# A two-layer spectral and dense block on one core: input rows spread over three DMA queues, the last slot of the spectral stage in halves of columns, and group 6's inverse steps moved ahead of the last group's third step

## The chip, the core and the metric

The kernel runs on one core of a Trainium2 chip. The metric is device time in microseconds (us) for one execution, taken as the median of several runs. Engines are named as in the profile: PE is TensorE, PEld its weight load, DVE VectorE, ACT ScalarE, POOL GpSimd, SP SyncE. SPq and ACTq are the DMA issues of SP and ACT.

## The reference

The input x has 2048 tokens of 1024 values. Two layers follow each other, each made of a spectral part A and a dense part B, with a layer norm ahead of each part and a residual after it:

```python
def _A_ref(x, w_r, w_i):
    B, S, D = x.shape
    X = rfft2(x.astype(float32))
    W = w_r + 1j * w_i
    return irfft2(X * W, s=(S, D)).astype(bfloat16)

def _B_ref(x, w1, b1, w2):
    h = einsum("bsd,df->bsf", x, w1) + b1
    sp = log1p(exp(-abs(h))) + where(h > 0, h, 0)
    return einsum("bsf,fd->bsd", h * tanh(sp), w2)

x = x + _A_ref(_layernorm(x), w_r, w_i)
x = x + _B_ref(_layernorm(x), w1, b1, w2)
x = x + _A_ref(_layernorm(x), w_r, w_i)
x = x + _B_ref(_layernorm(x), w1, b1, w2)
```

Here w_r and w_i are 2048 x 513, w1 is 1024 x 3584 and w2 is 3584 x 1024.

## The kernel before, in words

Every instruction is recorded by a small scheduler in Python: an engine has a list in the order in which the instructions are written, and waits are worked out from who wrote and read which buffer. So the order on an engine is the order of the source, and a wait holds everything behind it on that engine. DMAs (helper line L251) are issued by SP, ACT or POOL; the waits of a DMA hold the issuing engine.

**Prologue and s1.** SP issues the token tiles of x (XS, 13 transfers, one of them on ACT) and then x a second time in another layout, XR. XR has its rows in four quarters q of 32 column blocks; each quarter is eight transfers (h = 0 to 7) of 16 partitions x 32 runs of 256 bytes, 128 KB each. Even h is issued by SP, odd h by POOL after the last but two of the token tiles has landed. Meanwhile DVE and ACT compute the statistics of the layer norm (L471, L474, L452); a square root on ACT (`root`, L443) and a small transpose on PE (L595) turn them into scale factors. The matrix of the first transform step is then multiplied by these factors in 16 parts j, on ACT for j = 1 (L610), on POOL for j = 2, 4, 9, 10, 11, 13 and on DVE for the others (L616). Step s1 follows (L635): part j is eight matmuls into a pair of PSUM banks, which ACT (L641) or DVE (L643) copies out. Part j needs quarter j // 4 of XR. Three pairs of banks rotate. In the second layer, s1 takes another way to its rows and the prologue's transfers don't occur.

**The spectral steps.** The work is cut into eight groups g with two slots each. The steps of a group are 2 (`s2`, L742), 3 (`s3`, L787 to L790: four matmuls, a scaled copy on ACT at L794, and four DVE operations at L798, L800, L803, L805 that multiply by the filter), 4 (`i1`, L816: eight matmuls, copy out at L827) and 5 (`i2`, L841 and L873: copy out by ACT at L885 or DVE at L883). `order_A` writes the order of all steps by hand as three-digit words: step, group, slot or half. "371" is step 3 of group 7, slot 1. Each step takes the next of four pairs of PSUM banks in turn.

**The bounce through DRAM.** After both halves of step 5, `u_turn` writes the group's result to a scratch tensor (SP, 512 KB) and a later call reads it back with rows and columns exchanged (`u_back`, 16 partitions x 128 runs of 256 bytes, issued by SP). For group 7, each half is written by ACT as soon as it is there; `u_last` reads it back in six transfers: two of 8 partitions for the first half (SP), and four of 8 partitions, one for each quarter q, for the second half (q = 0, 2 on ACT; q = 1, 3 on SP).

**After the last step.** PE runs four `spin` matmuls (L652), eight matmuls of the residual (L1033) and a number of `hold` matmuls on a zero operand (L657; 16 in the first layer, 11 in the second), and then the last inverse step `i4` (L1044) quarter by quarter, each with a wait on that quarter's rows. Layer norm and the dense part (L1154, L1193, L1233, L1332) come after it.

Of the kernel before, what the change touches and what calls it, by code (L numbers as in the profile page):

```python
# [5 lines left out]
ACT = mybir.ActivationFunctionType  # L6
ALU = mybir.AluOpType
P = 128
# [172 lines left out]
class KB:  # L181
# [200 lines left out]
    def prologue(self):  # L382
        sp = self.sp
        self.op(self.pool, lambda e: e.memset(self.EPS[:], 1e-5), writes=[self.r_eps, self.r_warm])
        xt = self.x[0].rearrange("(t p) d -> p t d", p=P)

        for a, b in ((10, 11), (0, 1), (1, 2), (11, 12), (2, 3), (3, 4), (12, 13), (4, 6), (13, 14), (6, 8), (14, 15), (8, 10), (15, 16)):
            self.dma(self.act if a == 10 else sp, self.XS[:, a:b, :], xt[:, a:b, :], f"x{a}", writes=self.r_xs[a:b])
        self.warm(ACT.Sqrt)
        small = {}  # L390
        def load_small(name, n, d):
            b = self.alloc(name, self.o[name], [n], d)
            self.dma(sp, b.ap, self.con[name], name.lower(), writes=[b.res])
            small[name] = b
        load_small("M0", P, BF)
        load_small("IDF", P, F32)
        self.M0, self.IDF = small["M0"], small["IDF"]

        self.XR = self.alloc("XR", self.o["XR"], [P, P])
        self.r_xr = []  # L400
        xv = self.x[0].rearrange("(n2 n1) (h l) -> h n2 n1 l", n2=16, l=P)
        for q in range(4):
            r = Res(f"xr{q}")
            for h in range(8):
                prog = self.pool if h % 2 else sp
                self.dma(prog, self.XR.ap[h:P:8, 32 * q:32 * q + 32, :], xv[h][:, 32 * q:32 * q + 32, :], f"xr{q}{prog.name}",
                         parts=[r], reads=[self.r_xs[13]] if prog is self.pool else [])
            self.r_xr.append(r)
        self.dma(sp, self.FD[:], self.con["FD"], "fd", writes=[self.r_fd])
        load_small("JT", 4 * P, BF)  # L410
        self.JT, self.r_jt = small["JT"].ap, small["JT"].res
        self.w1_next = 0
# [168 lines left out]
    def first_scales(self):  # L581


        dve, act = self.dve, self.act
        for j in range(10):
            self.stats_dve(j)
        for j in range(10, 16):
            self.stats_act(j)
        self.sums_to_mv(10, 6)
        self.root(0, 16)  # L590
        rt = self.alloc("RT", self.o["RT"], [16, 8], F32)
        self.op(dve, lambda e: e.tensor_copy(rt.ap, self.RS[:, 2, :].unsqueeze(2).to_broadcast([P, 16, 8])),
                reads=self.r_rs, writes=[rt.res])
        bank = self.r_bank[7]
        self.group([lambda e: e.transpose(self.PS[:, 7, 0:P], rt.ap.rearrange("p a b -> p (a b)"), self.IDF.ap)],  # L595
                   reads=[rt.res, self.IDF.res], writes=[bank])
        self.op(dve, lambda e: e.tensor_copy(rt.ap.rearrange("p a b -> p (a b)"), self.PS[:, 7, 0:P]), reads=[bank], writes=[rt.res])
# [63 lines left out]
    def ring(self, name, n, size, shape):  # L661
        return [self.alloc(f"{name}{i}", self.o[name] + size * i, shape) for i in range(n)]
# [49 lines left out]
    def layer_A(self, li):  # L712
# [18 lines left out]
        def zslot(g, i):  # L731
            return Z[(2 * g + i) % 6]
# [48 lines left out]
        def s3(g, i):  # L781

            ps, banks, _ = self.pair()
            z, ft = zslot(g, i), FT[g % 3]
            t = ft.ap[:, i, :]
            fns = [
                lambda e: e.matmul(ps[:, 0:512], t[:, 0:128], z.ap[:, 0, :], start=True, stop=False),  # L787
                lambda e: e.matmul(ps[:, 512:1024], t[:, 0:128], z.ap[:, 1, :], start=True, stop=False),
                lambda e: e.matmul(ps[:, 512:1024], t[:, 128:256], z.ap[:, 0, :], start=False, stop=True),
                lambda e: e.matmul(ps[:, 0:512], t[:, 256:384], z.ap[:, 1, :], start=False, stop=True),  # L790
            ]
            self.group(fns, reads=[z.res, ft.res], writes=banks)
            x = X[(2 * g + i) % 4]
            self.op(act, lambda e: e.activation(x.ap.rearrange("p a b -> p (a b)"), ps, ACT.Copy, scale=SIG),  # L794
                    reads=banks, writes=[x.res])
            wt, yk = WT[(2 * g + i) % 8], YK[(2 * g + i) % 6]
            ta, tb = T[2 * i], T[2 * i + 1]
            self.op(dve, lambda e: e.tensor_tensor(ta.ap, x.ap, wt.ap[:, 0:1, :].to_broadcast([P, 2, 512]), ALU.mult),  # L798
                    reads=[x.res, wt.res], writes=[ta.res])
# [5 lines left out]
            self.op(dve, lambda e: e.tensor_tensor(yk.ap[:, 1, :], tb.ap[:, 0, :], ta.ap[:, 1, :], ALU.add),  # L805
                    reads=[ta.res, tb.res], parts=[yk.res])

        def i1(g, i):

            ps, banks, _ = self.pair()  # L810
            yk, bt, v = YK[(2 * g + i) % 6], BT[g % 3], V[g % 2]
            t = bt.ap[:, i, :]
            fns = []
            for c in range(4):
                for part in range(2):
                    fns.append(lambda e, c=c, part=part: e.matmul(  # L816
                        ps[:, c * 256:(c + 1) * 256], yk.ap[:, part, c * P:(c + 1) * P], t[:, (128, 0)[part]:(384, 256)[part]],
                        start=(part == 0), stop=(part == 1)))
            self.group(fns, reads=[yk.res, bt.res], writes=banks)
# [96 lines left out]

        def u_last():

            def back(prog, half, q, n):
                l = slice(32 * q, 32 * q + 32 * n)  # L920
                self.dma(prog, self.UT.ap[7 + 64 * half:P if half else 64:8, l, :], self.u_d[7][l, 8 * half:8 * half + 8, :].rearrange("l r n -> r l n"),
                         f"ul{half}{q}", reads=[self.r_ud7[half]], parts=self.r_ut[q:q + n])
            back(sp, 0, 0, 2)
            back(sp, 0, 2, 2)
            for q in range(4):
                back((act, sp)[q % 2], 1, q, 1)

        self.s1(li)
        if li:
# [5 lines left out]
        T = ring("T", 4, 2 * K, [2, 512])  # L935
        YK = ring("YK", 6, 2 * K, [2, 512])
# [41 lines left out]
    @staticmethod  # L978
    def order_A():


        order = ("200 201 210 211 300 301 220 310 400 221 311 401 230 320 410 500 231 321 411 501 330 331 420 510 240 511 421 241 "
                 "250 251 340 341 520 350 430 260 521 431 440 261 351 441 530 531 360 361 270 450 451 271 540 541 550 551 460 370 "
                 "461 371 560 561 470 471 570 571")
        return [tuple(map(int, w)) for w in order.split()]

    def load_wr(self, wr, g):
# [798 lines left out]
```

## Time and profile before

| | us |
|---|---|
| median of 3 runs (lowest, highest) | 928.16 (926.5, 930.47) |
| profiled span | 924.9 |
| PE busy | 878.7 (95%) |
| DVE busy | 622.9 (67%) |
| ACT busy | 434.8 (47%) |
| POOL busy | 157.5 (17%) |
| granted TensorE clock, mean | 0.998 |

Busy shares are averages over stages with different limits. Three stretches are touched by the change: the first 37 us, and the end of the spectral stage in each layer (about 85 to 112 us and 536 to 562 us from the span's start). In a timeline, each row gives the start, the busy time, the engine, the line, the operation, the number of instructions merged in the row, and in brackets how long the engine had been idle before it and what released it. In the chain of waits, each row gives the start, the length and the engine or transfer that set the pace. In the list of one line's instructions, the three numbers are shortest, median and longest duration in ns.

### The profile page before, as it was taken

What the parts mean: (1) busy time and instruction counts of PE and PEld (TensorE: products, weight loads), DVE (VectorE), ACT (ScalarE), POOL (GpSimd) and SP (SyncE); (2) the same over time, 40 slices, a digit from 0 to 9 for tenths busy, and PEclk for the clock granted to TensorE, in tenths of its full rate; (3) what the DMA queues carried; (4) which work ended last, traced back from release to release, by engine and by line L of the source; (5) the groups of instructions that cost most, each with busy time, mean ns of one, the idle gap of its engine ahead of it and who ended that gap; (6) DMA issues with size and microseconds to landing.
All of it is one profiled execution on the core that took longest, in us unless ns stands there. A gap on an engine that the chain in (4) does not pass through costs nothing.

```text
span 924.9 us, 13613 instructions
## 1 busy us (share of the span) xinstructions
PE 878.7 (95%) x5503; PEld 470.5 (51%) x5503; DVE 622.9 (67%) x987; ACT 434.8 (47%) x643; POOL 157.5 (17%) x186
## 2 busy tenths in 40 slices
PE   0899899999999999999998998999999999999998
PEld 0677576444444444444456766754444444444443
DVE  7898468686789667568867765666747655554463
ACT  7998475456103485520018966757550025552000
POOL 5831003960004651010121200000000000000000
PEclk9999999999999999999999999999999999999999
DMA  9979862674786388363723786345165635732432
GB/s 298 294 236 288 208 175 66 212 276 121 279 271 240 134 318 300 121 230 141 285 92 109 225 220 158 137 166 182 32 198 187 206 136 187 273 120 84 175 124 107
DMA packets 145919, 175.99 MB, mean 190 GB/s; under 512 B 66904, under 2 KB 124472, under 8 KB 145736
## 3 DMA queue, kind: packets, MB, share of 16 engines
q1 hardware_dynamic: 132960, 128.49, 44.6%
q0 software_dynamic: 10800, 45.00, 13.5%
q10 hardware_dynamic: 2096, 1.64, 0.6%
q8 instruction: 43, 0.70, 0.3%
q14 instruction: 20, 0.16, 0.1%
HBM read 130.78 MB, written 40.89 MB: 186 GB/s over the span
## 4 chain that ended last, share of the span: by engine, by line
PE 86%; DVE 6%; ACT 5%; DMA 2%; issue 1%; SPq 0%; ACTq 0%; DVEq 0%
PE PS L1332 37%; PE PS L1233 30%; PE PS L1193 6%; PE PS L742 3%; PE PS L816 2%; ACT ARENA L452 2%; PE PS L841 2%; PE PS L1044 2%; DMA ARENA<-u_scratch 1%; ACT ARENA L641 1%; PE PS L1154 1%; PE PS L652 1%; DMA u_scratch<-ARENA 1%; DVE ARENA L798 1%; DVE ARENA L800 1%; PE PS L873 1%
## 5 line engine op out<-in xcount | busy, mean ns | idle before, releaser
L1332 PE MATMUL PS<-ARENA 128*128 128x512 bf16 x1568 | 340.1, 379 | 0.0
L1233 PE MATMUL PS<-ARENA 128*128 128x512 bf16 (+1 forms) x1288 | 280.3, 379 | 0.8 <-DVE ARENA L1238 0.8
L1332 PEld LDWEIGHTS PS<-ARENA 128*128 128x128 bf16 x1568 | 153.2, 98 | 184.7 <-DMA ARENA<-in_B_w_dram 0.4
L1238 DVE TENSOR_TENSOR ARENA<-PS,ARENA 128x512 f32<-128x512 f32 x230 | 157.1, 691 | 100.4 <-PE PS L1233 92.6
L1233 PEld LDWEIGHTS PS<-ARENA 128*128 128x128 bf16 x1288 | 125.5, 98 | 153.1 <-DVE ARENA L1238 3.5
L1243 ACT ACTIVATE ARENA<-ARENA,B 128x512 bf16<-128x512 f32 x138 | 98.8, 721 | 69.1 <-DVE ARENA L1238 63.8
L574 ACT ACTIVATE ARENA<-PS 128x512 f32<-128x512 f32 (+3 forms) x86 | 61.6, 726 | 110.7 <-PE PS L1233 92.4
L1126 POOL TENSOR_TENSOR ARENA<-ARENA 128x512 bf16<-128x512 bf16 x56 | 71.3, 1272 | 77.1 <-DVE ARENA L523 63.6
L452 ACT ACTIVATE ARENA<-XS 128x1024 bf16<-128x1024 bf16 x60 | 63.2, 1053 | 36.3 <-DVE XS L1383 33.0
L1193 PE MATMUL PS<-ARENA 128*128 128x256 bf16 (+1 forms) x528 | 75.0, 300 | 3.4 <-DVE ARENA L1159 1.9
L1357 DVE TENSOR_TENSOR ARENA<-ARENA 128x3584 bf16<-128x3584 bf16 x32 | 63.9, 2017 | 0.0
L1193 PEld LDWEIGHTS PS<-ARENA 128*128 128x128 bf16 x528 | 51.0, 99 | 23.0 <-DVE ARENA L1159 3.3
L1383 DVE TENSOR_TENSOR XS<-PS,ARENA 128x512 bf16<-128x512 f32 x52 | 35.7, 690 | 38.7 <-PE PS L1332 38.4
L1375 DVE TENSOR_TENSOR ARENA<-PS,ARENA 128x512 f32<-128x512 f32 x48 | 32.9, 688 | 27.4 <-PE PS L1332 27.0
L1197 ACT ACTIVATE ARENA<-PS,B 128x256 bf16<-128x256 f32 (+1 forms) x66 | 33.2, 515 | 30.3 <-PE PS L1193 30.2
L1243 ACT ACTIVATE ARENA<-PS,B 128x512 bf16<-128x512 f32 x46 | 31.5, 685 | 18.4 <-PE PS L1233 18.4
L1371 DVE TENSOR_TENSOR ARENA<-ARENA,XS 128x512 f32<-128x512 f32 x52 | 36.8, 732 | 0.5
L443 ACT ACTIVATE RS<-MV,EPS 128x1 f32<-128x1 f32 (+2 forms) x11 | 3.3, 296 | 71.5 <-DVE MV L565 70.1
L794 ACT ACTIVATE ARENA<-PS 128x1024 bf16<-128x1024 f32 x32 | 32.5, 1046 | 5.1 <-PE PS L790 5.1
L816 PE MATMUL PS<-ARENA 128*128 128x256 bf16 x256 | 32.6, 273 | 1.4 <-DVE ARENA L805 1.4
L742 PE MATMUL PS<-FD,ARENA 128*128 128x256 bf16 (+1 forms) x256 | 31.4, 271 | 2.5 <-ACT ARENA L641 1.3
L1208 DVE TENSOR_TENSOR ARENA<-ARENA 128x2048 f16<-128x2048 bf16 x16 | 25.3, 1581 | 9.0 <-PE PS L1193 8.7
(100 smaller groups left out, 816.5 us busy)
## 6 DMA issues: line engine op xcount, KB each, us to landing
ARENA<-in_B_w_dram SPq DMA_DIRECT2D x30, 896.0 KB, 6.7
ARENA<-w1s_scratch SPq DMA_DIRECT2D x28, 896.0 KB, 4.6
ARENA<-w2s_scratch SPq DMA_DIRECT2D x24, 896.0 KB, 6.3
w1s_scratch<-ARENA POOLq DMA_DIRECT2D x14, 896.0 KB, 4.4
ARENA<-in_B_w_dram SPq DMA_DIRECT2D x24, 512.0 KB, 4.4
u_scratch<-ARENA SPq DMA_DIRECT2D x14, 512.0 KB, 4.7
ARENA<-u_scratch SPq DMA_DIRECT2D x14, 512.0 KB, 6.1
w2s_scratch<-ARENA POOLq DMA_DIRECT2D x8, 896.0 KB, 4.1
```

The source lines that it names most:

```text
L452: self.op(act, lambda e, i=i, f=f: e.activation(junk.ap, x, f, accum_out=sums[:, i:i + 1]), reads=[self.r_xs[j]], writes=[junk.res], parts ...
L574: fn = (lambda e: e.activation(dst, src, ACT.Copy)) if scale is None else \
L742: fns.append(lambda e: e.matmul(dst, at(r), FD[:, t:t + n], start=start, stop=stop))
L816: fns.append(lambda e, c=c, part=part: e.matmul(ps[:, c * 256:(c + 1) * 256], yk.ap[:, part, c * P:(c + 1) * P], t[:, (128, 0)[part]:(384, ...
L1126: self.op(self.pool, lambda e, dst=A(dst), x=A(x), y=A(y), op=op: e.tensor_tensor(dst, x, y, op), reads=[b.res] + list(after), writes=[b.rs])
L1193: fns.append(lambda e, db=db, bank=bank, fl=fl: e.matmul(PS[:, bank, 0:w], wb.ap[:, db, fl * P:(fl + 1) * P], x.ap[:, db, tok], start=(db ...
L1233: self.group([lambda e, db=db: e.matmul(PS[:, bank, :], A[:, db, :], mov[:, db, :], start=(start and db == 0), stop=(db == 3), skip_group_ ...
L1238: self.op(dve, lambda e: e.tensor_tensor(dst.ap, PS[:, bank, :], x.ap, ALU.add), reads=[self.r_bank[bank], x.res], writes=[dst.res])
L1243: self.op(act, lambda e: e.activation(at, src, ACT.Mish, bias=self.B1[:, ft:ft + 1]), reads=[res, self.r_b1], writes=[ra])
L1332: self.group([lambda e, i=i, k=k, b=PB[n][k].ap: e.matmul(PS[:, bank, :], ap[:, i, t * P:(t + 1) * P], b[:, i - 7 * k, :], start=(start an ...
L1357: self.op(dve, lambda e: e.tensor_tensor(ap[dst][:, f, :], ap[x][:, f, :], ap[y][:, f, :], op), reads=part(x, k) + part(y, k), writes=part ...
L1371: self.op(dve, lambda e: e.tensor_tensor(a[t], a[t], x, ALU.add), reads=[rx], writes=[r[t]])
```

## The change

The change has four parts.

1. **Rows over three queues.** Quarters 0 and 2 of XR are issued wholly by SP; of quarters 1 and 3, SP issues even h; odd h of quarter 1 is issued by POOL, after quarter 0 has landed; odd h of quarter 3 is issued by ACT, right after the square root (`late_rows`). SP then has 24 of these transfers instead of 16, POOL 4 instead of 16, ACT 4 instead of none. It is for getting the first quarter in without other rows beside it.
2. **Last slot in halves.** For slot 1 of group 7, the copy on ACT, the four DVE operations and the matmuls of `i1` are made for 256 of the 512 columns, and then for the other 256, so that `i1` can begin on the first half.
3. **Order.** Group 6's `i1` steps (460, 461) come ahead of group 5's step 5, and 560 ahead of 370, 561 ahead of 371. It is for having group 6 out of the way before the last group.
4. **Read-back of group 7.** Four transfers of 16 partitions (both halves together; q = 0, 1 on ACT, q = 2, 3 on SP) take the place of six of 8 partitions.

```diff
+        self.r_xr = [Res(f"xr{q}") for q in range(4)]
+
+        def rows(q, h, prog):
+            self.dma(prog, self.XR.ap[h:P:8, 32 * q:32 * q + 32, :], xv[h][:, 32 * q:32 * q + 32, :], f"xr{q}{prog.name}",
+                     parts=[self.r_xr[q]], reads=self.r_xr[:1] if prog is self.pool else [])
         for q in range(4):
-            r = Res(f"xr{q}")
             for h in range(8):
-                prog = self.pool if h % 2 else sp
-                self.dma(prog, self.XR.ap[h:P:8, 32 * q:32 * q + 32, :], xv[h][:, 32 * q:32 * q + 32, :], f"xr{q}{prog.name}",
-                         parts=[r], reads=[self.r_xs[13]] if prog is self.pool else [])
-            self.r_xr.append(r)
+                if h % 2 == 0 or q not in (1, 3):
+                    rows(q, h, sp)
+                elif q == 1:
+                    rows(q, h, self.pool)
+        self.late_rows = lambda: [rows(3, h, self.act) for h in (1, 3, 5, 7)]
...
         self.root(0, 16)
+        self.late_rows()
...
+            if (g, i) == (7, 1):
+                halves(x, wt, yk, ta, tb, ps, banks)
+                return
...
+            for k in range(2):
+                c = slice(256 * k, 256 * k + 256)
...
+                self.op(act, lambda e, c=c: e.activation(x.ap[:, :, c], src[:, :, c], ACT.Copy, scale=SIG), reads=banks,
+                        writes=[rx], parts=[x.res])
+                for t, rt, n in ((ta, ra, 0), (tb, rb, 1)):
+                    self.op(dve, lambda e, c=c, t=t, n=n: e.tensor_tensor(t.ap[:, :, c], x.ap[:, :, c], wt.ap[:, n:n + 1, c].to_broadcast([P, 2, 256]),
+                                                                          ALU.mult), reads=[rx, wt.res], writes=[rt], parts=[t.res])
+                for n, (a, b, op) in enumerate(((ta, tb, ALU.subtract), (tb, ta, ALU.add))):
+                    self.op(dve, lambda e, c=c, n=n, a=a, b=b, op=op: e.tensor_tensor(yk.ap[:, n, c], a.ap[:, 0, c], b.ap[:, 1, c], op),
+                            reads=[ra, rb], writes=[ry] if n else [], parts=[yk.res])
...
+            if (g, i) == (7, 1):
+                for k in range(2):
+                    self.group(fns[4 * k:4 * k + 4], reads=[last_yk[k], bt.res], writes=banks[k:k + 1])
...
-            back(sp, 0, 0, 2)
-            back(sp, 0, 2, 2)
             for q in range(4):
-                back((act, sp)[q % 2], 1, q, 1)
+                l = slice(32 * q, 32 * q + 32)
+                self.dma((act, act, sp, sp)[q], self.UT.ap[7:P:8, l, :], self.u_d[7][l, :, :].rearrange("l r n -> r l n"),
+                         f"ul{q}", reads=self.r_ud7, parts=self.r_ut[q:q + 1])
...
-                 "250 251 340 341 520 350 430 260 521 431 440 261 351 441 530 531 360 361 270 450 451 271 540 541 550 551 460 370 "
-                 "461 371 560 561 470 471 570 571")
+                 "250 251 340 341 520 350 430 260 521 431 440 261 351 441 530 531 360 361 270 450 451 271 540 541 460 461 550 551 "
+                 "560 370 561 371 470 471 570 571")
```

More of the change, by code (lines that the diff above doesn't have):

```diff
@@ L793, in s3 @@
             x = X[(2 * g + i) % 4]
+            wt, yk = WT[(2 * g + i) % 8], YK[(2 * g + i) % 6]
+            ta, tb = T[2 * i], T[2 * i + 1]
+            if (g, i) == (7, 1):
+                halves(x, wt, yk, ta, tb, ps, banks)
+                return
             self.op(act, lambda e: e.activation(x.ap.rearrange("p a b -> p (a b)"), ps, ACT.Copy, scale=SIG),
                     reads=banks, writes=[x.res])
-            wt, yk = WT[(2 * g + i) % 8], YK[(2 * g + i) % 6]
-            ta, tb = T[2 * i], T[2 * i + 1]
             self.op(dve, lambda e: e.tensor_tensor(ta.ap, x.ap, wt.ap[:, 0:1, :].to_broadcast([P, 2, 512]), ALU.mult),
@@ L806, in s3, with halves @@
                     reads=[ta.res, tb.res], parts=[yk.res])
+        last_yk = []
+        def halves(x, wt, yk, ta, tb, ps, banks):
+            src = ps.rearrange("p (a b) -> p a b", a=2)
+            for b in (x, ta, tb, yk):
+                b.res.begin()
+            for k in range(2):
+                c = slice(256 * k, 256 * k + 256)
+                rx, ra, rb, ry = (Res(f"{n}h{k}") for n in ("x", "ta", "tb", "yk"))
+                last_yk.append(ry)
+                for r, b in ((rx, x), (ra, ta), (rb, tb), (ry, yk)):
+                    r.inherit(b.res)
+                self.op(act, lambda e, c=c: e.activation(x.ap[:, :, c], src[:, :, c], ACT.Copy, scale=SIG), reads=banks,
[6 more added lines that the diff above has]
+                            reads=[ra, rb], writes=[ry] if n else [], parts=[yk.res])
+            for b in (x, ta, tb):
+                b.res.r(dve, dve.count)
         def i1(g, i):
@@ L818, in i1 @@
                         start=(part == 0), stop=(part == 1)))
-            self.group(fns, reads=[yk.res, bt.res], writes=banks)
+            if (g, i) == (7, 1):
+                for k in range(2):
+                    self.group(fns[4 * k:4 * k + 4], reads=[last_yk[k], bt.res], writes=banks[k:k + 1])
+                yk.res.r(self.pe, self.pe.count)
+            else:
+                self.group(fns, reads=[yk.res, bt.res], writes=banks)
             if i == 0:
@@ L917, in u_last @@
         def u_last():
[L919 to L922, printed above, removed]
-            back(sp, 0, 0, 2)
-            back(sp, 0, 2, 2)
             for q in range(4):
-                back((act, sp)[q % 2], 1, q, 1)
+                l = slice(32 * q, 32 * q + 32)
+                self.dma((act, act, sp, sp)[q], self.UT.ap[7:P:8, l, :], self.u_d[7][l, :, :].rearrange("l r n -> r l n"),
+                         f"ul{q}", reads=self.r_ud7, parts=self.r_ut[q:q + 1])
         self.s1(li)
```

## The prediction

> **What bounds the kernel now.** I read the page first. Its shares by engine, and the shares by engine of the chain that ended last, say that TensorE sets the time nearly everywhere:
>
> ```profile
> PE 878.7 (95%) x5503; PEld 470.5 (51%) x5503; DVE 622.9 (67%) x987; ACT 434.8 (47%) x643; POOL 157.5 (17%) x186
> ...
> PE 86%; DVE 6%; ACT 5%; DMA 2%; issue 1%; SPq 0%; ACTq 0%; DVEq 0%
> ```
>
> So only some 46 us are PE idle, and the change touches three short stretches of them. For the first I read the chain of waits between 20 and 46 us:
>
> ```profile
> 21.36 2.45 ACT ARENA L610 x8
> ...
> 23.86 1.05 PE PS L635 x8
> 24.93 3.78 ACT ARENA L641 x4
> ```
>
> The reader should see ACT: its eight scalings for j = 1 release PE, then its copies of s1 set the pace. Rows of x appear nowhere in it. The timeline of the same stretch shows what ACT did just before:
>
> ```profile
> 19.54 0.31 ACT L443 ACTIVATE RS<-MV,EPS 128x16 f32<-128x16 f32 x1 [0.64 <-DVE MV L465]
> ...
> 21.36 2.44 ACT L610 ACTIVATE ARENA<-ARENA 128x128 bf16<-128x128 bf16 x8 [1.51 <-DVE ARENA L597]
> ```
>
> ACT is free for 1.51 us only, from 19.85 to 21.36. The one wait of PE for rows is 0.42 us at 27.01 (quarter 1), and the chain passes it by, since ACT was still copying.
>
> For the end of the spectral stage I read the chain of the second layer:
>
> ```profile
> 542.95 0.93 ACT ARENA L794
> ...
> 543.90 0.69 DVE ARENA L798
> ...
> 548.05 1.06 PE PS L816 x8
> ...
> 551.65 2.31 DMA u_scratch<-ARENA
> ...
> 556.01 5.38 DMA ARENA<-u_scratch
> ...
> 561.43 2.58 PE PS L1044 x96
> ```
>
> From 542.95 on it is a latency chain: ACT copies group 7's slot 0, DVE multiplies slots 0 and 1 back to back (543.90 to 548.0), PE does i1 and i2, the result goes to DRAM and back, and PE takes it. The first layer has the same chain (91.78, 92.73, 96.87, then 4.32 us of write from 101.53 and 4.20 us of read from 105.87). But PE is filled meanwhile with spin, residual and hold matmuls, and the timeline shows how little it waits at the end: 0.85 us ahead of L1044 at 110.31 in the first layer, and 0.57 us at 561.43 (second quarter) in the second.
>
> **What the Trainium skill says.** "DMA: Bandwidth & Descriptors", section "Why a DMA increments its semaphore by 16 and not by 1": a DMA uses at most as many engines as divide its slowest dimension, so one over 8 rows runs on 8 of 16. The trace agrees: while the 8-partition reads of group 7 ran (106 to 110 us) it shows about 105 GB/s, and about 285 GB/s in the stretches filled with 16-partition reads of the same 256-byte runs. Section "Issuing engines are not separate DMA queues" of that page: issuing from several engines saves only issuing time. The trace agrees as far as rates go: 315 GB/s at 13 to 15 us with SP's queue nearly alone, 290 to 268 GB/s with POOL's beside it. Section "Queues, rings and completion order": each engine takes packets from its queues in turn. At 15 to 17 us POOL's queue moved 0.50 MB in 175 packets, SP's 0.08 MB in 317, so large packets win.
>
> **Part 1, rows.** Four issues are put on ACT behind the square root, hence ahead of L610. SP's issues of this same transfer take 627 ns at least, POOL's 625. ACT's nearest row, "478.13 2.75 ACTq" for four transfers beside SP and POOL, gives 0.69 each. Four at 0.627 from 19.85 end at 22.4 instead of 21.36: +1.05 us. Bounds: at ACT's shortest issue (0.326, a write to scratch) they fit into the gap, +0; at its longest (1.174) they end at 24.5, +3.2. I take 1.05. Queued behind them are L610, which PE's part 1 waits for, and all of L641. From 23.7 to 35.1 ACT copies with gaps of 0.2 us, so nothing takes the delay back and all of it passes to step 2 at 36.57.
>
> Arrival of rows: the token tiles end near 13.7 us. SP then has four row transfers in its ring and issues one each 0.627 us, so the eighth starts at 14.0 + 3 x 0.627 = 15.9 and lands 2.8 to 3.0 us later (the latency of SP's last rows before), near 19. POOL then issues four in 2.5 us, to 21.5, when its L616 begins anyway (21.41), and they land 5.8 us after their issue, near 26.7. Part j = 4 needs them at 26.6 + 1.05. The whole 4.2 MB at 270 GB/s from 13.7 end near 29.3, plus latency 31; part 12 needs quarter 3 near 33. So the rows cost nothing by themselves and bring nothing: the removed 0.42 us wait was not on the chain.
>
> **Parts 2 and 3, together.** I lay out PE's steps from 536.92 (second layer) with the trace's durations: i1 and s3 0.87, i2 0.87 + 0.99, ACT copy 0.93 to 1.03, DVE 2.0 per slot. New order: 540, 541 to 538.9; 460, 461 to 540.6; 550, 551 to 542.5; 560 to 543.4; 370 to 544.25 (before: 542.6). ACT has copied 560 by 544.4 and copies slot 0 to 545.4 (before 543.9), copies 561, then slot 1 in two halves of 0.60 (the row of L574 for 512 columns). Slot 0's DVE work ends at 547.4. Halves on DVE: 1024 elements cost 0.689, 512 cost 0.420; the step is 0.27, so 256 cost about 0.29. Back to back, with 0.08 us overlap, a half is 0.34 + 0.42 + 0.21 + 0.21 = 1.18 against 2.0 for a whole slot. The halves end at 548.55 and 549.7 (before: 548.0). i1's first half (0.44) is hidden, the second ends at 550.2 (before: 549.1). DVE's copy for slot 0 (L578, 0.69) now stands behind the halves on DVE's queue, ending at 550.4, and the copy for slot 1 ends at 551.1 against 549.83. So 570 starts 1.3 us later: +1.65 from moving 370 back, -0.35 from the halves. The first layer gives +1.35 in the same way. The filler of PE starts that much later.
>
> Group 6's write gains nothing: in the trace SP was held at 542.21 for 2.12 us by its full ring, then read groups 4 and 5 for 3.95 us, and issued group 6's write only at 548.36, long after its data. The new order makes the data earlier, not the queue.
>
> **Part 4, read-back.** Half 1 brought 256 KB and half 0 256 KB, both at about 105 GB/s. Now 512 KB come in one piece, at 285 GB/s 1.84 us, plus 2.0 to 2.8 latency: all lands about 4.2 us after the write, quarter 0 after 3.3 (before: 4.2 for the first quarter in layer one, 5.4 from the issue of the second quarter in layer two). Hence PE's filler becomes the bound. First layer: filler took 7.93 us (101.53 to 109.46), so L1044 starts at 101.53 + 1.35 + 7.93 = 110.8 against 110.31: +0.5. Second layer: 552.7 + 1.3 + 6.72 = 560.75 for the first quarter against 559.46, but the 0.57 wait at the second is gone: +0.7. Write: if it landed as late as 4.3 us after 102.9, quarter 0 would be there at 110.5, still in time.
>
> Sum: 1.05 + 0.5 + 0.7 = +2.25 us. 928.16 + 2.25 = 930.4.
>
> **Rivals.**
> Faster: the read-back was the real bound, and the compute chain is not longer, because PE's order leaves slack I misjudge. Then 0.85 + 0.57 = 1.4 us go, and if ACT's issues also fit into its 1.51 us gap, the time is 926.7. For it: both waits are seen, and the 105 GB/s. Against: DVE is continuous over both slots, and 370 is moved behind three more steps.
> Slower on the start: ACT's issues are held (+3.2), or POOL's odd rows of quarter 1 land late. One landing of 13.2 us and one of 10.5 us are in the trace; 20.9 + 10.5 = 31.4 against a need at 27.7 would be +3.7. Either, with +1.2 of the two tails, gives +4.4 to +4.9: about 933. For it: large packets crowd others out. Against: then POOL's were the large ones, and here POOL's are the awaited.
> Slower in the tails: the write or SP's read of group 6 collides with the later group 7, and the first quarter comes 1 us after the filler in both layers: +2 more, 932.4.
>
> **How the numbers follow.** Forecast 0.58 (930.4), faster rival 0.17 (926.7), late rows or held ACT 0.15 (933), late tails 0.10 (932.4). Runs of before spread by 2 us to either side of the median. The range from 925.5 to 934.0 takes in the cases and this spread, and leaves out about 2 in 10. The bound of 0.5% is 4.6 us. Faster by that needs more than all waits named: 0.05. Slower by that needs the late rows with an end of the spread: 0.13. Within: 0.82.
>
> **What would show it.** Part 1: an ACTq row of four transfers between 19.9 and 22.4 and L610 starting near 22.4; it fails if L610 stays at 21.36, or starts after 23.5. Rows: no wait of PE for rows over 0.5 us. Parts 2 and 3: 1.6 us more from 541's end to slot 0's L794, eight DVE operations of about 0.42 and 0.29 us, and 570 1.3 us later relative to 540; it fails if 570 is not later. Part 4: 250 to 290 GB/s during the read-back and no wait ahead of L1044. The prediction is wrong if PE waits for rows or for group 7's read by over 1 us, or if the stage from 36.57 on shrinks.

## The result and the profile after

The changed kernel takes 932.73 us (median; 930.35 to 934.45) against 928.03 us (926.5 to 930.47) for the kernel before: a ratio of 1.0047, interval 1.0025 to 1.0068. That is 4.4 us longer by the ratio, 2.3 to 6.3 us by its ends. The prediction had 930.4 us: longer by 2.25 us. The mean granted clock of the changed kernel was 0.998 or 1.000 in all six executions, and the three at 1.000 took 930.5 to 934.5 us, so a lower clock is not what made it longer.

After the change, line numbers are moved: L610, L616 and L635 are now L616, L622 and L641; step 2 (L742) is L748; the ACT copy of step 3 (L794) is L805, its DVE operations L807 to L814 for whole slots and L833, L836 for halves; `i1` (L816) is L849, step 5 (L841, L873) is L879, L911, spin is L658 and `i4` (L1044) is L1078. Each experiment has numbers of its own.

Busy times and the shares of the chain that ended last hardly differ from before:

```profile
PE 875.7 (94%) x5426; PEld 472.4 (51%) x5503; DVE 623.5 (67%) x995; ACT 435.5 (47%) x645; POOL 150.2 (16%) x174
...
PE 85%; DVE 6%; ACT 5%; DMA 1%; issue 1%; ACTq 0%; DVEq 0%
```

PE has no more to do: its weight loads are 5503 in both, and the 77 matmuls by which after is short of that number are records missing from the trace. It waits a little more. The place has to be found by marks in the timeline, in us from the start of the span:

| mark | before | after | later by | added since the last mark |
|---|---|---|---|---|
| ACT's eight scalings for j = 1 | 21.36 | 22.66 | 1.30 | +1.30 |
| first matmul of step 2 | 36.57 | 39.44 | 2.87 | +1.57 |
| first layer: 540 | 85.55 | 89.96 | 4.41 | +1.54 |
| 570 | 98.71 | 104.83 | 6.12 | +1.71 |
| `i4` | 110.31 | 116.57 | 6.26 | +0.14 |
| second layer: 540 | 536.92 | 541.39 | 4.47 | -1.79 |
| 570 | 549.88 | 556.05 | 6.17 | +1.70 |
| `i4`, second quarter | 561.43 | 566.87 | 5.44 | -0.73 |
| end of the span | 924.9 | 930.3 | 5.4 | 0 |

The +1.54 and the -1.79 are not the change's. In the windows by stretch the granted clock of after is 0.79 at 36 to 44 us, that of before 0.86 at 118 to 130 us; each is 1.00 in the other profile. Such dips occur in some executions of either kernel (the part-1 kernel below, with the same start as after, has 1.00 at 36 to 44; two kernels with the start of before have 0.79). The rest falls where the change is: the start, and the two tails (a tail is the stretch from 540, the first half of step 5 of group 4, to `i4`).

**Start.** The timeline of after:

```profile
19.67 0.31 ACT L448 ACTIVATE RS<-MV,EPS 128x16 f32<-128x16 f32 x1 [0.64 <-DVE MV L470]
19.68 2.88 ACTq L251 DMA_DIRECT2D ARENA<-in_A_x_dram  x4
...
22.66 2.44 ACT L616 ACTIVATE ARENA<-ARENA 128x128 bf16<-128x128 bf16 x8 [2.68 <-DVE ARENA L622]
...
25.16 2.74 PE L641 MATMUL PS<-ARENA 128*128 128x128 bf16 x24 [1.39 <-ACT ARENA L616]
```

The four issues stand between ACT's square root and its scalings. The bracket of L616 names DVE, but DVE's operation had begun at 21.40 and the issues ended at 22.56: it is they that held ACT. PE's second part then waits 1.39 us for L616 (0.25 before).

**Tail of the second layer.** The chain of waits of after:

```profile
549.17 0.92 ACT ARENA L805
...
550.12 0.69 DVE ARENA L807
...
554.67 0.62 PE PS L849 x4
555.29 0.02 issue
555.31 0.61 ACT ARENA L579
555.92 0.14 issue
556.05 1.47 PE PS L879 x12
...
567.04 2.40 PE PS L1078 x96
```

The DMA rows that stood in this chain before (write 2.31, read 5.38) are gone: behind 570 there is PE, and one copy on DVE. The read-back no longer sets the end here, but 570 itself starts 14.66 us after 540 (12.96 before).

**Tail of the first layer.** Here the chain of after has the DMA rows still:

```profile
107.66 5.39 DMA u_scratch<-ARENA
...
113.12 3.21 DMA ARENA<-u_scratch
116.33 0.25 issue
116.57 0.95 PE PS L1078 x32
```

The read of the first quarter is shorter, 3.21 us against 4.20. The write before it is longer, 5.39 against 4.32. The timeline shows what lies beside it:

```profile
106.81 0.53 SPq L251 DMA_DIRECT2D ARENA<-u_scratch  x1
107.66 0.33 ACTq L251 DMA_DIRECT2D u_scratch<-ARENA  x1
...
116.57 0.95 PE L1078 MATMUL PS<-MT,ARENA 128*128 128x32 bf16 x32 [1.00 <-DMA ARENA<-u_scratch]
```

SP issued its 512 KB read of group 6 at 106.81, ahead of the second write of group 7 at 107.66; before, it came 1.07 us behind it (102.60 and 101.53). PE waits 1.00 us for the read-back, more than the 0.85 us that the change was to take away.

### The profile page after: what moved, and what is told of

It is laid out like the page before. It is cut to its first block, busy times and chain, and to the rows that moved or that the text cites. A ratio compares the mean times of both kernels' runs of the same rounds, so it can differ in the third digit from the quotient of the medians.

```text
span 930.3 us, 13539 instructions
## 1 busy us (share of the span) xinstructions
PE 875.7 (94%) x5426; PEld 472.4 (51%) x5503; DVE 623.5 (67%) x995; ACT 435.5 (47%) x645; POOL 150.2 (16%) x174
## 4 chain that ended last, share of the span: by engine, by line
PE 85%; DVE 6%; ACT 5%; DMA 1%; issue 1%; ACTq 0%; DVEq 0%
PE PS L1366 36%; PE PS L1267 29%; PE PS L1227 6%; ACT ARENA L457 2%; PE PS L849 2%; PE PS L748 2%; PE PS L879 2%; PE PS L1078 2%; PE PS L641 1%; PE PS L1188 1%; PE PS L658 1%; DVE ARENA L807 1%; PE PS L911 1%; ACT ARENA L647 1%; DVE ARENA L809 1%
## 5 line engine op out<-in xcount | busy, mean ns | idle before, releaser
L1267 PE MATMUL PS<-ARENA 128*128 128x512 f16 (+1 forms) x1265 | 279.0, 379 | 2.0 <-DVE ARENA L1272 0.8
L849 PE MATMUL PS<-ARENA 128*128 128x256 bf16 x256 | 32.8, 273 | 5.1 <-DVE ARENA L814 3.6
L748 PE MATMUL PS<-FD,ARENA 128*128 128x256 bf16 (+1 forms) x256 | 32.8, 279 | 2.5 <-ACT ARENA L647 1.3
L805 ACT ACTIVATE ARENA<-PS 128x1024 bf16<-128x1024 f32 x30 | 30.2, 1036 | 5.0 <-PE PS L796 5.0
```

The source lines that it names most:

```text
L748: fns.append(lambda e: e.matmul(dst, at(r), FD[:, t:t + n], start=start, stop=stop))
L849: fns.append(lambda e, c=c, part=part: e.matmul(ps[:, c * 256:(c + 1) * 256], yk.ap[:, part, c * P:(c + 1) * P], t[:, (128, 0)[part]:(384, ...
L1267: self.group([lambda e, db=db: e.matmul(PS[:, bank, :], A[:, db, :], mov[:, db, :], start=(start and db == 0), stop=(db == 3), skip_group_ ...
```

## The experiments

All kernels compute the whole result. Microseconds are the ratio's distance from 1, times the 927.5 to 928.2 us of the kernel before that ran beside it.

| kernel | ratio (95%) | us |
|---|---|---|
| e1_rows: part 1 alone | 1.0014 (1.0002 to 1.0025) | +1.3 |
| e3_act_issue: ACT's four issues alone | 1.0013 (1.0004 to 1.0022) | +1.2 |
| e4_rows_no_act: part 1, POOL in ACT's place | 1.0027 (1.0017 to 1.0037) | +2.5 |
| e2_tail: parts 2 to 4 | 1.0028 (1.0012 to 1.0044) | +2.6 |
| e5_order: part 3 alone | 1.0082 (1.0059 to 1.0105) | +7.6 |
| e6_halves: part 2 alone | 1.0000 (0.9984 to 1.0016) | 0 |
| e7_read: part 4 alone | 0.9980 (0.9969 to 0.9991) | -1.9 |
| e8_halves_read: parts 2 and 4 | 0.9989 (0.9976 to 1.0002) | -1.0 |
| e9_order_fill: order, PE's waits filled | 1.0039 (1.0024 to 1.0055) | +3.6 |
| e11_after_gate: after, group 6's read held | 1.0063 (1.0049 to 1.0078) | +5.8 |
| e10_trim: read-back, fewer hold matmuls | 0.9978 (0.9968 to 0.9989) | -2.0 |
| e12_trim_fill: e10 and dummy matmuls | 0.9970 (0.9962 to 0.9979) | -2.8 |

The first question was which half of the change costs: the start or the tails.

**e1_rows** is the kernel before with part 1 of the diff, unchanged.

> The kernel before with the rows over three queues only (part 1). If the start makes most of the loss, as the changed kernel's trace has it (2.9 us more up to step 2, of which 1.3 by ACT held by its four issues, 0.4 by quarter 1 landing late, 1.2 by matmuls that run at 0.10 instead of 0.063 us), the time is 2.5 to 3.5 us above before, and more where the granted clock drops at 39 to 42 us again. If the tails make it, it is at most 1.3 us above before. My blind forecast for this part alone was +1.05.

It gave +1.3 us. Its ACT issues take 2.94 us and L616 starts at 23.11, 1.75 later than before, of which 0.52 is a later square root in that execution (20.06 against 19.54).

**e2_tail** is the kernel before with parts 2, 3 and 4.

> The kernel before with parts 2, 3 and 4 only (halves, order, read-back), its start left as it was. The changed kernel's trace has the two tails 1.85 and 0.95 us longer: +2.8 if that holds without the start, and s1 as before. If the tails only looked longer because the start was late (other transfers shifted), the time is within 1 us of before. My blind forecast for these parts was +1.2.

It gave +2.6 us. 570 starts 14.85 us after 540 in the first layer and 14.66 in the second, as in after (14.87 and 14.66). In the first layer the write takes 5.11 us, the read 3.54, and PE waits 1.05 us. So the two halves add up (1.3 + 2.6 = 3.9, within the interval of the whole), and both lose.

**e3_act_issue** takes only the issuing engine out of part 1:

```diff
             for h in range(8):
+                if q == 3 and h % 2:
+                    continue
                 prog = self.pool if h % 2 else sp
...
+        self.late_rows = lambda: [self.dma(self.act, self.XR.ap[h:P:8, 96:128, :], xv[h][:, 96:128, :], "xr3ACT", parts=[self.r_xr[3]])
+                                  for h in (1, 3, 5, 7)]
...
         self.root(0, 16)
+        self.late_rows()
```

> The kernel before with one edit: the four odd transfers of quarter 3 are issued by ACT behind the square root instead of by POOL. It prices ACT's issues alone. If ACT is held in order by its issues, L610 starts at 22.5 to 22.7 instead of 21.36, and all of s1 ends 1.1 to 1.3 us later with the rows of quarter 1 still in time. If issues cost ACT nothing, L610 stays at 21.4.

Its timeline:

```profile
19.69 2.71 ACTq L251 DMA_DIRECT2D ARENA<-in_A_x_dram  x4
...
22.50 2.45 ACT L615 ACTIVATE ARENA<-ARENA 128x128 bf16<-128x128 bf16 x8 [2.51 <-issue]
```

Here the bracket itself says "issue". The scalings come 1.14 us late, of which 0.14 is a later square root in that execution (19.68 against 19.54), and the kernel loses 1.2 us: as much as all of part 1. The issues on ACT alone are enough to account for its cost, within the intervals.

**e4_rows_no_act** is the opposite: the rows of part 1, but POOL issues the odd rows of quarters 1 and 3.

```diff
-                elif q == 1:
+                else:
                     rows(q, h, self.pool)
-        self.late_rows = lambda: [rows(3, h, self.act) for h in (1, 3, 5, 7)]
+        self.late_rows = lambda: [rows(3, h, self.act) for h in ()]
```

> Part 1 with ACT left out: POOL issues the odd rows of quarters 1 and 3, all behind the landing of quarter 0 (eight issues), SP the rest. If ACT's issues are the cost, L610 is back at 21.4 and the time within 0.8 us of before. If the late quarter 1 is the cost, PE still waits ahead of part j = 4 to about 28.5 and its matmuls stay slow, and POOL's scalings begin 2.5 us later still (about 25), which holds parts 2 and 4 too: 2 to 4 us above before.

It gave +2.5 us, worse than with ACT:

```profile
19.61 5.13 POOL L251 DMA_DIRECT2D ARENA<-in_A_x_dram  x8 [18.75 <-DMA ARENA<-in_A_x_dram]
...
21.52 2.44 ACT L616 ACTIVATE ARENA<-ARENA 128x128 bf16<-128x128 bf16 x8 [1.52 <-DVE ARENA L603]
...
24.84 5.60 POOL L622 TENSOR_TENSOR ARENA<-ARENA 128x1024 bf16<-128x1024 bf16 x3
...
26.80 3.48 PE L641 MATMUL PS<-ARENA 128*128 128x128 bf16 x29 [1.74 <-POOL ARENA L622]
```

ACT is back at 21.52, but POOL now spends 5.13 us on issues that wait for quarter 0, its own scalings start at 24.84 instead of 21.41, and PE waits 1.74 us for POOL. So the issues have only moved from one engine that is needed at this moment to another. The kernel before is quicker since POOL there issues its rows while it has nothing else to do.

For the tails the question was which of the three parts loses.

**e5_order** changes only the order string.

> The kernel before with the new order of steps only (part 3). If moving slot 0 of group 7's third step back is what lengthens the tails, 570 starts 1.6 to 2.0 us later after 540 than before in both layers, the write of group 7's second half then meets SP's read of group 6, and the time is 2 to 3.5 us above before. If the halves or the new read-back are to blame, it is within 0.5 us of before.

It gave +7.6 us, far more than any theory had. The marks explain only part: 570 starts 14.90 us after 540 in the first layer (13.16 before) and 15.13 in the second (12.96). The windows by stretch of the second layer show the other part (PE, PEld, DVE, ACT, POOL; then granted clock, DMA share, GB/s):

```profile
553.00:563.00 10.00, 8.42 (x42) 4.20 (x43) 2.61 (x4) 1.79 (x3) 0.00 (x0) 0.52 0.77 203
```

The fields are length, then busy us and instructions of each engine. The clock is 0.52, and the timeline shows step 5 of group 7 at about half speed, 2.74 us instead of 1.48, behind waits of PE of 1.33, 0.95 and 0.79 us ahead of 470, 471 and 570:

```profile
555.25 2.74 PE L841 MATMUL PS<-ARENA,BD 128*128 128x256 bf16 x12 [0.79 <-DVE ARENA L578]
```

This is more than one execution's accident. Five of the six executions of this kernel have a mean granted clock of 0.991 to 0.995; the sixth has 1.000 and is the quickest, 932.24 us, still about 4 us above the kernel before. None of the 51 executions of the kernel before that ran beside it is under 0.996.

**e6_halves** is part 2 alone.

> The kernel before with the last slot in halves only (part 2). By the rows of DVE (two halves 2.4 us against 2.0 for a slot, i1's end 0.44 behind the last operation instead of 1.05) 570 starts 0.2 to 0.4 us earlier, or not at all earlier if DVE's copies for slot 0, now behind the halves, end last: time within 0.5 us of before, either way.

It shows no change: 1.0000, with 1.5 us of room to either side. 570 starts 13.11 and 12.92 us after 540, a gain of 0.05 us.

**e7_read** is part 4 alone.

> The kernel before with the read-back of group 7 in four transfers of 16 partitions only (part 4). If the 16-partition form is the faster one, the first quarter lands 3.2 to 3.6 us after the write, both waits of PE (0.85 and 0.57 us) go, and the time is 1.0 to 1.5 us below before. If the larger transfers only queue longer, the waits stay or grow by up to 0.5 us each: 0 to 1 us above before.

It gave -1.9 us, a gain whose interval is clear of 1. The timeline of its first layer:

```profile
106.45 1.48 ACTq L251 DMA_DIRECT2D ARENA<-u_scratch  x2
106.46 3.66 PE L657 MATMUL PS<-BD,ARENA 128*128 128x512 bf16 x16
...
110.21 0.95 PE L1040 MATMUL PS<-MT,ARENA 128*128 128x32 bf16 x32
```

There is no bracket on L1040: the first quarter is there when the hold matmuls end. From 570 to `i4` it takes 10.85 us (11.60 before), and from 570 to the second quarter in the second layer 10.79 (11.55 before). That is 0.75 and 0.76 us less, 1.5 together: about the two waits of 0.85 and 0.57 us that the profile of before showed.

**e8_halves_read** has parts 2 and 4.

> Parts 2 and 4 with the old order and the old start. If the order is the whole loss of the tails and the read-back a gain, this is 1 to 1.8 us below before, the best of the combinations. If the halves cost something together with the read-back, it is above the read-back alone.

It gave -1.0 us, with an interval that reaches to no change and overlaps that of e7_read. The halves add nothing to the read-back that shows.

Now two causes were left to test: the clock behind the order, and SP's read of group 6.

**e9_order_fill** is e5_order with matmuls that fill PE's waits; their results are overwritten by the real ones.

```diff
+            if g == 7:
+                self.group([lambda e: e.matmul(ps[:, 0:512], BD[:, 0:P], BD[:, 0:512], start=True, stop=True)] * (5, 3)[i],
+                           reads=[self.r_bd], writes=banks)
             self.group(fns, reads=[yk.res, bt.res], writes=banks)
...
+            if g == 7 and half == 0:
+                self.group([lambda e: e.matmul(ps[:, 0:512], BD[:, 0:P], BD[:, 0:512], start=True, stop=True)] * 3,
+                           reads=[self.r_bd], writes=banks)
```

> The new order only, with 11 dummy matmuls in each layer (5 ahead of 470, 3 ahead of 471, 3 ahead of 570), where PE waits. The order alone was 7.3 us above before in its median, though its steps lengthen the tails by 1.7 and 2.0 us only; its profile shows matmuls at half speed in three places, one of them in these very waits of the second layer. If the waits make PE lose its clock, the dummies bring the time down by 1.5 to 4 us, to 931.5 to 934, with a granted clock of 1.00 between 540 and 570 us. If the loss of clock is chance and not tied to the waits, the time stays at 935 or rises by up to 0.5 us.

It gave +3.6 us where the order alone had +7.6; the intervals don't overlap. The same window as above:

```profile
553.00:563.00 10.00, 8.09 (x45) 3.36 (x44) 1.29 (x2) 1.19 (x2) 0.00 (x0) 1.00 0.70 159
```

and the timeline:

```profile
552.26 1.48 PE L844 MATMUL PS<-ARENA,BD 128*128 128x256 bf16 x12
```

Here step 5 comes earlier in the window, but the clock is 1.00 over the whole execution as well, step 5 takes 1.48 us, and none of this kernel's nine executions has a mean clock under 0.996. Eleven matmuls per layer that compute nothing give back about half of what the order costs. (The two kernels ran at different times, each beside the kernel before.) The other half is the longer tail itself: 570 still starts 14.91 and 14.72 us after 540, about 1.8 us later in each layer than before.

**e11_after_gate** is the changed kernel with SP's read of group 6 held until both writes of group 7 have landed:

```diff
-                if half == 0:
-                    u_back(6)
...
-        def u_back(g):
+        def u_back(g, more=()):
...
-                     reads=[self.r_ud[g]], parts=self.r_ut)
+                     reads=[self.r_ud[g]] + list(more), parts=self.r_ut)
 
         def u_last():
+            u_back(6, self.r_ud7)
```

> The changed kernel with one edit: SP's read-back of group 6 (512 KB) waits until both writes of group 7 have landed. If that read is what makes the write of group 7's second half take 5.4 us in the first layer (4.3 before, 2.0 to 2.3 in the second layer), the write takes 3 to 4 us now, while the reads behind it take about 1.8 us longer: time within 1 us of the changed kernel. If group 6's write or something else is at fault, the write stays at 5 us and the time rises by about 1.5 to 2 us in each layer.

The timeline of its first layer:

```profile
106.48 0.33 ACTq L251 DMA_DIRECT2D u_scratch<-ARENA  x1
...
108.84 2.73 SPq L251 DMA_DIRECT2D ARENA<-u_scratch  x3
108.85 1.48 ACTq L251 DMA_DIRECT2D ARENA<-u_scratch  x2
```

The write landed 2.29 us after its issue. All profiles taken together, by the place of SP's read of group 6:

| read of group 6 | tails | the last write takes, us |
|---|---|---|
| issued ahead of the write (after, e2, e5, e9) | 8 | 3.3 to 5.4 |
| issued behind it (before, e1, e6, e7, e8, e10, e12) | 14 | 2.0 to 4.5 |
| held until it has landed (e11) | 2 | 2.0 and 2.3 |

Between after and e11 only this read differs, and the write falls from 5.39 and 3.36 us to 2.29 and 1.99: the read ahead of it is what lengthens it. Of the eight tails in the first row, those of the first layer take 4.65 to 5.4 us and those of the second 3.3 to 4.5; why the first layer is the longer isn't shown. The kernel gains nothing by holding the read: its interval overlaps that of after, since now the held read is in the way of the read-back. `i4` of the first layer starts 10.57 us after 570 instead of 11.74, but in the second layer the read-back takes 5.29 us, and from 570 to the second quarter it takes 11.46 us instead of 10.82. The 512 KB have to pass either ahead of the write or beside the last read.

**e10_trim** is e7_read with `hold(7 if li else 14, 7)` instead of `hold(11 if li else 16, 7)`, since the earlier read-back needs less to bridge.

> The kernel before with the 16-partition read-back (part 4) and fewer hold matmuls: 14 instead of 16 in the first layer and 7 instead of 11 in the second. With the read-back alone PE ran hold to 110.1 and 557.7 us with the data there, so each matmul taken away (0.216 us) should come back: 0.4 + 0.9 us less than the read-back alone, about 3 us below before. If the reads land only just in time, PE waits for them instead and the time is that of the read-back alone.

It gave -2.0 us, the same as e7_read. PE waits 0.54 us for the read in the first layer (`i4` at 109.97) and 1.44 us in the second: filler and transfer are about equally long, so trimming filler turns it into waiting.

**e12_trim_fill** is e10_trim with three dummy matmuls ahead of 570 and four `spin` matmuls ahead of the dense part of the first layer, for the clock:

```diff
+            if g == 7 and half == 0:
+                self.group([lambda e: e.matmul(ps[:, 0:512], BD[:, 0:P], BD[:, 0:512], start=True, stop=True)] * 3,
+                           reads=[self.r_bd], writes=banks)
...
+        self.spin(4, 0)
         for fg in range(4):
             mm1(0, fg, 0, mid=turns(0, 2, 3) if fg == 3 else ())
```

> The run with fewer hold matmuls, with dummy matmuls in two waits of PE that are left: 3 ahead of 570 in each layer and 4 ahead of the dense part of the first layer, where the profile of before had PE at half speed from 119.2 to 122.8 us (1.6 us lost). If such waits cost clock in a part of the executions, the median falls by another 0.5 to 1.5 us and the slow end of the runs comes nearer. If not, it is within 0.3 us of the run without them.

925.27 us against 928.15 (0.9970): the quickest of all, and below both kernels. Against e10_trim (925.58) the difference is within the intervals, so what is shown is the read-back's gain; that the dummy matmuls add to it isn't.

## Why the prediction was right or wrong

Its direction held, and so did the time: 932.73 is in the range of 925.5 to 934.0, and the change is within 0.5% by its middle, though the interval goes beyond. The range held in part by its width, since the spread of single runs alone was given 2 us to either side. The sum was too small by half: 2.25 against 4.4 (2.3 to 6.3). What it lacks is mostly in the tails, 2.8 us by the marks where 1.2 was forecast, and 1.00 us of that is one wait for the read-back. By steps:

**Part 1, ACT's issues: right.** "+1.05" was worked out from 0.627 us per issue. Single issues took 0.65 to 0.66 us in the median, the four together 2.71 to 2.94 us with the gaps between them, and they cost 1.2 us (e3_act_issue). L616 at 22.66 is close to "near 22.4". Two small misses cancel here: the issues were longer than forecast, but the first began beside the square root (19.68), not after its end (19.85). That the whole delay passes on is borne out by the medians; single profiles scatter too much for it, as is shown below.

**Part 1, rows: right in what they bring, wrong in the working.** They neither bring nor cost anything that the medians show (+1.3 with them, +1.2 without). But the rate of 270 GB/s failed. The DMA view at 15 to 21 us, and SP's issues in the same stretch, before:

```profile
DMA packets 2517, 1.69 MB, mean 282 GB/s; under 512 B 2231, under 2 KB 2231, under 8 KB 2517
...
q0 software_dynamic: 426, 1.17, 70.3%
...
L251 SPq DMA_DIRECT2D ARENA<-in_A_x_dram x5: 627/955/2296, 15.0 to 19.8; - x5
```

and after:

```profile
DMA packets 4379, 1.09 MB, mean 181 GB/s; under 512 B 4379, under 2 KB 4379, under 8 KB 4379
...
L251 SPq DMA_DIRECT2D ARENA<-in_A_x_dram x10: 627/628/629, 14.9 to 20.9; - x10
...
DMA to landing us min/median/max: 2.9/3.1/6.1
```

Before, POOL and SP issue side by side, and SP is held by its full ring for up to 2.3 us at an issue. After, SP issues alone until 19.7 us, one transfer straight after the other, and most land about 3 us later, so hardly anything queues. In the windows 15 to 17 and 17 to 19 us the rate is 172 and 185 GB/s, with a DMA share of 0.79 and 0.82, against 290 and 269 GB/s with 1.14 and 1.12 before. So here the pace of one issuing engine sets the rate. The prediction had that pace, 128 KB each 0.627 us, which is 209 GB/s at most (my estimate from its own two numbers), and took 270 GB/s beside it all the same. POOL's packets are larger, 2.7 KB on average (1.17 MB in 426) against 250 bytes for SP's. How much that adds is not tested; at 27 to 29 us of after, with nearly all packets of 256 bytes but rows of several engines under way, the rate is 263 GB/s, so small packets alone don't hold it at 181. The last rows landed at 34.2 us instead of "31".

Quarter 0 landed at 19.44, somewhat later than "near 19". POOL's issues, which wait for it, ran until 22.38 instead of 21.5, so POOL's scalings began at 22.49 and not at 21.41; PE didn't wait for them in after, but in e4_rows_no_act it does. Quarter 1 was complete with POOL's last transfer at 28.62, 6.9 us after its issue, instead of "near 26.7", and PE paused 0.81 us until 28.71, where the prediction allowed 0.5. Kernels with the old start show anything from no wait to 0.98 us there.

Why the start in the profile of after lost 2.87 us, when e1_rows costs 1.3, is answered by the mean duration of a matmul. At 29 to 31 us, before:

```profile
L635 PE MATMUL PS<-ARENA 128*128 128x128 bf16 x32 | 2.3, 219 | 0.4 <-ACT ARENA L641 0.3
```

and after:

```profile
L641 PE MATMUL PS<-ARENA 128*128 128x128 bf16 x21 | 2.4, 311 | 0.0
```

PE begins slow and becomes quick at about 27.0 us in before and 32.7 in after, though the clock column says 1.00 throughout. The Trainium skill, "TensorE: Matmul & The Clock Gate", section "What's actually happening", says that PE runs at half clock until it has been busy through a window of about 3.4 us, and that the windows run freely, so the moment varies by about 0.5 us to either side. The trace agrees with the two levels: in before, 24 of these matmuls took 2.74 us at 23.86 and 1.52 at 27.02. The moment varies by far more here: in nine profiles of kernels with the old start it lies between 26.0 and 32.5 us, though the first matmul always starts at 22.6 to 22.9; the measurement decides. The page speaks of sustained activity, and here PE waits in between; that this is the reason is not tested. Step 2 begins between 36.57 and 38.53 us in these nine (middle 37.01); with part 1 it begins at 38.27, 38.91 and 39.44. So one profile of this stage says little on a change of 1 us, and the prediction took its starting point from the earliest of them.

**Part 2, halves: right in the DVE times, wrong in what they bring.** The eight operations took 0.42 and 0.29 us as predicted, and both halves 2.40 us (100.91 to 103.31) against 2.36. The "-0.35" for 570 was 0.05 (e6_halves). Both numbers can be found again in the profiles: from the end of DVE's work to 570 it takes 1.52 us in after and 1.89 in before, a gain of 0.37, but DVE takes 2.40 us for the two halves and 2.09 for the whole slot, which costs 0.31 of it. In the chain above, 570 waits for the copy of the second half's bank on ACT (555.31, 0.61) behind the last matmul of `i1`: the halves move the start of `i1`, and the end hangs on the last half, which isn't earlier.

**Part 3, order: right in size, with one cost missing.** 570 was to start 1.3 to 1.35 us later. It starts 1.71 and 1.70 later. The order by itself gives 1.74 (e5_order, first layer), close to the predicted 1.65; what is too small is the saving by the halves. Missing altogether was the clock: where the order left PE three waits in a row, the granted clock fell, and the order cost 7.6 us, where with filled waits it cost 3.6. In the change itself this did not show: with the halves, PE's waits are 1.33, 0.15, 0.59 and 0.78 us with work between them, and 553 to 563 us has a clock of 1.00. That the halves are what saves it is argued from e5_order, e2_tail and these waits; a run of order and halves without the read-back, which could tell the halves from the read-back as the reason, is missing.

**Part 4, read-back: right in the second layer, wrong in the first.** PE's filler as the new bound came as predicted in e7_read and in the second layer of after. So did the first quarter, "3.3": 3.2 us in both layers of after and 3.5 in the first layer of e7_read; in the second layer of e7_read, where the read of group 6 is still under way, it took 4.3. The step that failed is "if it landed as late as 4.3 us after 102.9, quarter 0 would be there at 110.5, still in time". The write takes 5.39 us, since group 6's read is now issued ahead of it: against before, the read moved by 4.21 us (102.60 to 106.81) and the write by 6.13 (101.53 to 107.66). In the second layer the read is ahead too, by 0.60 us (558.27 and 558.87), but there the write took 3.36 us, and PE's filler still covered it. The first layer was to lose 1.35 - 0.85 = 0.5 and lost 1.71 + 0.14 = 1.85; the second was to lose 0.7 and lost 1.70 - 0.73 = 0.97. Together 2.8 against 1.2; e2_tail has 2.6.

So the third rival, late tails by a collision of the write with group 6's read, is what happened, in one layer of two: it named 1 us of wait there, and 1.00 us was measured. I gave it 0.10. That its sum, 932.4, is so near the measured 932.73 is partly luck, since it had this wait in both layers. The prediction's own signs say the same: "no wait ahead of L1044" failed in the first layer, and 1.00 us is at its mark of "over 1 us" for being wrong; "no wait of PE for rows over 0.5 us" failed at the start, though kernels with the old start fail it too. A hint was in the profile of before: the write of the first layer's second half, with the read of group 6 issued 1.07 us behind it, took 4.32 us. It was no more than a hint, because in the second layer the read was issued 0.64 us behind the second write and that one took 2.00 us at most.

**What stays open.** In which executions and at which place the clock dips is not settled: two of the 22 executions of e8_halves_read, which has the old order, have a mean clock of 0.993 and 0.994 too. Nor is the sum of the tails' parts (0 + 7.6 - 1.9 is 5.7, and together they cost 2.6).

## What to carry to other kernels

A DMA issue of 128 KB kept the issuing engine for 0.63 to 0.66 us here, so look at what stands behind it on that engine, not only at where the queue has room, and work out what one engine can issue before counting on a rate that two had reached. Before moving work so that a latency-bound write comes later, list what else the queues will hold at that moment. And when a change makes TensorE's waits longer, look at the granted clock too: in e9_order_fill, matmuls that do nothing were cheaper than the waits.

## What was not expected of the hardware

- A wait can cost TensorE more than its length: after waits of 1.33, 0.95 and 0.79 us within some 6 us, twelve matmuls took 2.74 us instead of 1.48 and the granted clock was 0.52 over 10 us; with 11 dummy matmuls per layer in the waits it was 1.00, and the kernel 4 us shorter. Five of six executions without them had a mean clock of 0.991 to 0.995, none of nine with them was under 0.996.
- At the start of the kernel, matmuls of 128 columns took 310 to 314 ns until some moment between 26 and 33 us, and 219 ns afterwards, while the clock column showed 1.00.
- A 256 KB write took 2.0 to 2.3 us with SP's 512 KB read of 256-byte runs held back. It took 5.1 to 5.4 us in the first layer of after, e2_tail and e5_order, with that read issued 0.5 to 0.9 us ahead of it, and 3.3 to 4.65 in the other tails with the read ahead.
- The same rows went in packets of 2.7 KB on average when POOL issued them and of 256 bytes from SP and ACT.
- At 15 to 19 us, with SP issuing alone, 128 KB about each 0.67 us, the rows came at 172 and 185 GB/s; with SP and POOL issuing side by side, at 290 and 269. The Trainium skill, "DMA: Bandwidth & Descriptors", section "Issuing engines are not separate DMA queues", says that issuing from several engines saves only the time to issue, which it calls small as a rule. Here that time was what counted: as SP's pace at the start, and on ACT, where it was spent and not saved.
